# Eight tiles or six transposed on TensorE: tiles 6 and 7 moved to DMA transposes, with a new written order

## The chip, the cores and the metric

The kernel runs on one core of one Trainium2 chip. The metric is the device time of one execution in microseconds, the median of three runs.

## What is computed

Attention with four batches, eight heads, 768 positions and a head width of 64, in which each position sees the first 8 positions and the last 96 up to itself, followed by a two-layer network with a squared ReLU:

```python
scores = scale * np.matmul(q, k.transpose(0, 1, 3, 2))
keep = is_global | is_local          # pos < 8, or 0 <= rel < 96
bias = -slopes[:, None, None] * dist[None, :, :]
a = softmax(np.where(keep, scores + bias, -1e9))
attn = np.matmul(a, v)               # (4, 8, 768, 64)
x = attn.transpose(0, 2, 1, 3).reshape(3072, 512)
h = x @ w_in                         # (3072, 2048)
g = np.maximum(h, 0.0) ** 2
out = g @ w_out                      # (3072, 512)
```

## The kernel before

The 3072 rows are cut into 24 tiles of 128 (`j`, six for each batch) and 12 blocks of two tiles (`blk`). Because a position sees at most 96 back, a tile's scores need only its own keys and those of the tile before it; the first 8 keys and values of a batch are copied into each later tile (`gk`, `gv`, or a copy `kl`).

The program first builds a list of operations (`Plan.op`), each with the engines that may do it, and then emits them one after the other in the sequence that the string `ORDER` gives (`Plan.run`). A word of `ORDER` is the name of an operation; `:` is followed by the PSUM banks that it takes, `@A`, `@V` or `@P` picks ACT, DVE or POOL, `#2` the second operation of that name. Each engine works through its own operations strictly in this sequence, so `ORDER` is the order of PE, ACT, DVE, and of the two lines of transfers, POOL's and SP's. Nothing else sets it: the planner's keys and costs in the code are not used for the order. Numbers such as `LEADS` and `key=` only describe.

The operations, in the course of a tile:

- `ld.q.j`, `ld.k.j`, `ld.v.j`, `ld.win.s.c`, `ld.wout.s` (line 307) and `load.j` (line 310: v, q and k of tile j, from tile 6 on) are loads issued by POOL, with the cast to bf16. q and k of tile 0 come from SP as float32 (`plain`, line 319). The weights are loaded in eight steps `s` of 256 columns or rows; steps 0 and 2 of w_in in two halves.
- `tr.0.j` and `tr.1.j` (line 506) transpose q and k of tile j on PE, four 128x128 transposes each, and `T.0.j`, `T.1.j` (lines 429 to 433) copy them from a bank to `qkT`. This holds for `j < JQK`. For later tiles `T.j` (line 537) is one DMA transpose of q and k together, issued by SP.
- `bias.j` (line 579, first three tiles) and `sc.j` (line 599) fill the banks with scores, `exp.j` (line 665, ACT) and `mul.j` (line 690, DVE) make the weights, `pv.j` (line 748) multiplies with v, `norm.j` (lines 778 and 779, DVE) divides.
- `trx.j` (line 816) and `xT.j` (lines 429 to 433) transpose the result x on PE for `j < JX`; for later tiles `xT.j` (line 840) is a DMA transpose issued by SP.
- `s1` and `relu`, `sq` (lines 1061, 865, 1098) are the first layer for blocks 0 and 1. From block 2 on it is done by seven products of half size in place of eight: `isum` and `xs` (lines 888 and 922) are sums of weights and inputs, `h` (line 950) the products, `u`, `c` and `q` what ACT and DVE make of them.
- `s2.0` (line 1339) is the second layer for block 0, with `w_out` step by step; from block 1 on it is seven products too: `wsum` and `sum` (lines 1132 and 1167) are sums of w_out and hidden values, `s2.blk.p1` to `p7` (line 1212) the products, `part` and `o` (lines 429 and 1287) what collects them, `st` (lines 1309 and 1381) the stores, issued by SP.
- `warm` (line 532) is eight matmuls of zeros. The same eight run once at the very start (line 372).

The waits that matter around the change: `s2.0.s.sub` waits for `ld.wout.s`, `wsum.i.g` for four steps of w_out, `isum.i.g` for the transposes `tr` of all tiles of the first loads and for four steps of w_in, `T.j` for the landing of `load.j`, and `load.j` for the transposes that free its place in the ring of three q and k buffers.

Of the kernel before, what the change touches and what calls it, by code (L numbers as in the profile page):

```python
# [77 lines left out]
isum.1.0 T.8 s2.0.6.1 u.2.1.2@A s2.0.6.0 isum.3.0 pv.6.1:0 h.2.0.p6 wsum.2.1 wsum.0.1 s2.1.p1.1 s2.0.7.1 c.2.1.c11
norm.6.0 gate.13 o.0.1@V st.0.1 s2.0.7.0 h.2.1.p7 part.1.p1@A s2.1.p6.0 u.2.0.2@A o.0.0@A u.2.1.3@A h.2.0.p7 h.2.1.p4
T.9 norm.6.1 wsum.3.0 u.2.0.3@A sc.7.0:1762 c.2.1.c21@A wsum.1.1 h.2.1.p5:0 c.2.1.c22 q.2.1.c11@A s2.1.p2.0:4  # L80
exp.7.1.0 exp.7.0.0 isum.2.1 load.10 h.2.0.p4 exp.7.0.1 mul.7.0 exp.7.1.1 s2.1.p2.1 isum.2.0 s2.2.p1.0:7 q.2.1.c21@A
mul.7.1 h.2.0.p5:1 s2.1.p6.1 part.1.p6@A trx.6:6 gate.12 c.2.0.c21@A load.12 pv.7.0:2 xT.6@A c.2.0.c22 q.2.1.c22@A
q.2.0.c22@A s2.2.p1.1 h.2.1.p3 s2.1.p7.0 wsum.3.1 o.1.p2 norm.7.0 h.2.0.p3 pv.7.1:5 s2.1.p7.1 q.2.0.c21@A st.0.0
c.2.1.c12 s2.1.p5.0 s2.1.p5.1 part.1.p7@A q.2.1.c12@A s2.1.p4.0 T.10 s2.1.p4.1 c.2.0.c12 gk.7@V q.2.0.c12@A o.1.p5
o.1.p4@A sc.8.0:6201 st.1.1 part.2.p1@A s2.1.p3.0 norm.7.1 sum.2.0 sum.2.1 s2.1.p3.1 trx.7:5 xT.7@V o.1.p3 h.3.0.p1:3
exp.8.1.0 gk.8@V h.3.1.p1:2 exp.8.0.0 exp.8.1.1 exp.8.0.1 h.3.0.p2:6 xs.3.0 u.3.1.1@A sc.9.0:1540 s2.2.p6.0 mul.8.0
xs.3.1 mul.8.1 u.3.0.1@A h.3.0.p6 exp.9.0.1 exp.9.1.1 gv.7@V h.3.1.p2:4 c.3.0.c11 h.3.1.p6 c.3.1.c11 exp.9.0.0
pv.8.0:0 s2.2.p6.1 pv.8.1:6 load.11 norm.8.0 u.3.1.2@A s2.2.p2.0:1 sum.2.2 gv.8@P q.3.1.c11@A norm.8.1 xT.8 h.3.1.p7
h.3.0.p5:4 u.3.0.2@A h.3.0.p7 s2.2.p2.1 exp.9.1.0 st.1.0 part.2.p6@A xs.3.2 u.3.1.3@A q.3.0.c11@A h.3.1.p5:0 s2.2.p7.0
u.3.0.3@A mul.9.1 mul.9.0 s2.2.p7.1 c.3.1.c22 T.12 c.3.0.c22 pv.9.0:6 h.3.1.p3 o.2.p2 h.3.0.p4 c.3.1.c12 load.15  # L90
norm.9.0 q.3.1.c22@A h.3.0.p3 s2.3.p1.0:5 s2.3.p1.1 c.3.0.c12 q.3.0.c22@A pv.9.1:0 c.3.0.c21@A part.2.p7@A norm.9.1
q.3.1.c12@A h.3.1.p4 q.3.0.c12@A h.4.0.p1:3 c.3.1.c21@A s2.2.p5.0 part.3.p1@A gk.9@V sc.10.0:6402 s2.2.p5.1
q.3.0.c21@A sum.3.0 sum.3.1 s2.2.p4.0 s2.2.p4.1 exp.10.1.0 sum.2.3 exp.10.0.0 exp.10.0.1 h.4.0.p2:4 T.11 u.4.0.1@A
exp.10.1.1 gk.10@V gv.9@A s2.3.p6.0 o.2.p5 mul.10.0 c.4.0.c11 xT.9 h.4.1.p1:6 o.2.p4@A mul.10.1 s2.2.p3.0 s2.2.p3.1
q.3.1.c21@A s2.3.p2.0:0 sum.3.2 u.4.1.1@A pv.10.0:2 pv.10.1:4 s2.3.p6.1 xs.4.0 gate.17 o.2.p3 part.3.p6@A xs.4.1
s2.3.p2.1 norm.10.0 h.4.0.p6 h.4.1.p6 q.4.0.c11@A gv.10@A norm.10.1 u.4.0.2@A load.13 s2.3.p7.0 sc.11.0:7124 u.4.1.2@A
sum.3.3 h.4.0.p7 h.4.1.p7 xs.4.2 exp.11.1.0 o.3.p2 exp.11.0.0 u.4.0.3@V s2.3.p7.1 sc.12.0:17 exp.11.1.1 exp.11.0.1
gate.16 xT.10 h.4.0.p4 c.4.0.c21@A mul.11.0 st.2.0 mul.11.1 h.4.1.p2:4 c.4.1.c11 exp.12.1.0 s2.3.p5.0 pv.11.0:2
pv.11.1:3 s2.3.p5.1 norm.11.0 part.3.p7@A h.4.0.p5:7 q.4.1.c11@A u.4.1.3@A norm.11.1 h.4.1.p5:4 q.4.0.c21@A gate.20
s2.3.p4.0 c.4.0.c22 load.14 s2.3.p4.1 h.4.0.p3 T.13 gate.18 load.16 c.4.1.c22 exp.12.0.0 h.4.1.p4 q.4.1.c22@A h.4.1.p3  # L100
xT.11 s2.4.p2.0:2 h.5.0.p1:3 q.4.0.c22@A o.3.p5 mul.12.0 c.4.0.c12 o.3.p4@A c.4.1.c21@A u.5.0.1@A c.4.1.c12 T.15
s2.3.p3.0 q.4.0.c12@A s2.3.p3.1 q.4.1.c12@V q.4.1.c21@A h.5.0.p2:1 o.3.p3 sc.13.0:5764 st.3.1 st.2.1 h.5.1.p1:0
exp.13.0.0 T.14 s2.4.p2.1 c.5.0.c11 exp.13.1.0 pv.12.1:1 q.5.0.c11@A s2.4.p1.0:5 xs.5.0 sum.4.0 pv.12.0:7 xs.5.1
s2.4.p1.1 mul.13.0 h.5.0.p6 gk.13@V u.5.1.1@A exp.13.0.1 h.5.1.p6 exp.13.1.1 h.5.0.p5:6 sum.4.1 norm.12.0 norm.12.1
h.5.1.p2:4 xs.5.2 mul.13.1 c.5.1.c11 h.5.1.p5:7 u.5.1.2@A sum.4.2 gate.19 part.4.p1@A h.5.1.p7 u.5.0.2@A h.5.0.p7
o.4.p2 u.5.0.3@A c.5.0.c22 pv.13.0:1 u.5.1.3@A norm.13.0 s2.4.p6.0 s2.4.p6.1 xT.12 st.3.0 q.5.1.c11@A T.16 part.4.p6@A
h.5.0.p4 pv.13.1:4 s2.4.p5.0 sum.4.3 c.5.0.c21@A h.5.0.p3 h.5.1.p4 q.5.0.c22@A s2.4.p7.0 norm.13.1 s2.4.p7.1 s2.4.p5.1
c.5.0.c12 q.5.0.c21@A kl.15@V part.4.p7@A c.5.1.c22 q.5.0.c12@A sc.14.0:1346 o.4.p5 s2.4.p4.0 xT.13 exp.14.0.1 kl.14@V
h.5.1.p3 gv.13@P q.5.1.c22@V c.5.1.c12 c.5.1.c21@A s2.4.p4.1 load.17 h.6.0.p1:4 s2.4.p3.0 s2.4.p3.1 exp.14.1.1
exp.14.1.0 exp.14.0.0 sc.15.0:0673 mul.14.1 mul.14.0 xs.6.0 o.4.p4@A xs.6.1 h.6.0.p2:1 o.4.p3 q.5.1.c12@A s2.5.p1.0:5  # L110
u.6.0.1@A c.6.0.c11 exp.15.0.0 exp.15.1.0 exp.15.1.1 sum.5.0 s2.5.p1.1 h.6.0.p6 u.6.0.2@A exp.15.0.1 sum.5.1 load.18
h.6.0.p5:2 part.5.p1@A pv.14.0:0 norm.14.0 pv.14.1:6 h.6.1.p1:1 u.6.1.1@A h.6.0.p7 gv.14@P st.4.0 s2.5.p6.0 u.6.0.3@A
# [1319 lines left out]
```

## Time and profile before

| what | value |
|---|---|
| three runs | 199.76, 199.83 and 200.56 us |
| median | 199.83 us |
| span of the profiled execution | 197.6 us |
| instructions of PE, ACT, DVE, POOL in it | 2776, 335, 423, 101 |
| busy time of PE, DVE, ACT, POOL | 191.9, 173.2, 163.0, 80.4 us |
| loads by POOL (q0) | 13.37 MB in 80256 packets |
| stores and transposes by SP (q1) | 13.11 MB in 31570 packets |

The span runs from the first to the last instruction of one profiled execution; the page gives no other time for that execution, and the median of the runs is 2.2 us above the span. A matmul's shown time runs on into the next one's, so the step from one start to the next tells what a matmul costs, and the chain of waits gives these steps added up. In a timeline the columns are start, duration, engine, line and operation, what is written and read with its shape, the count of merged instructions, and in brackets the idle time before and what ended it. An issue of a transfer is shown on POOL or SP; its landing is told by the DMA view, as a median time from issue.

### The profile page before, as it was taken

The page shows a single profiled execution, that of the slowest core. Times are in us where ns is not written, and L with a number is a line of the kernel's source. Part 1 is how long each engine was busy: PE and PEld are TensorE (multiplying, and loading weights), DVE is VectorE, ACT ScalarE, POOL GpSimd, SP SyncE. Part 2 cuts the span into 40 slices and gives each one's busy share as a digit, 9 for nine tenths or more (in the row PEclk, how much of TensorE's full clock was granted, in tenths as well). Part 3 has the DMA queues.
Part 4 walks back from the last instruction along what each step waited for, and adds up shares of the span by engine and source line. Part 5 has one row for each costly group of instructions (what it writes and reads, how often), then busy time and mean ns, then how long its engine had stood idle before and what let it go on. Part 6 is the DMA issues. An engine that isn't in the chain of part 4 may idle for free.

```text
span 197.6 us, 6777 instructions
## 1 busy us (share of the span) xinstructions
PE 191.9 (97%) x2776; PEld 169.6 (86%) x2776; DVE 173.2 (88%) x423; ACT 163.0 (82%) x335; POOL 80.4 (41%) x101
## 2 busy tenths in 40 slices
PE   7989999999999999999999999999999999999993
...
DMA  6999999999999999999999999999695711114023
GB/s 127 153 158 171 181 181 185 182 202 159 139 209 191 75 200 88 145 174 210 151 129 203 114 124 194 160 121 92 136 81 116 154 55 56 27 30 163 0 106 106
DMA packets 111857, 26.91 MB, mean 136 GB/s; under 512 B 103379, under 2 KB 109011, under 8 KB 111827
## 3 DMA queue, kind: packets, MB, share of 16 engines
q0 software_dynamic: 80256, 13.37, 91.8%
q1 hardware_dynamic: 31570, 13.11, 32.5%
q8 instruction: 21, 0.34, 0.6%
q14 instruction: 10, 0.07, 0.1%
...
## 4 chain that ended last, share of the span: by engine, by line
PE 95%; DVE 2%; issue 1%; ACT 0%; DVEq 0%
PE bank L1212 35%; PE bank L950 32%; PE bank L1061 7%; PE bank L599 6%; PE bank L748 5%; PE bank L1339 4%; PE bank L372 2%; PE bank L506 2%; PE bank L532 1%; DVE qkT L433 1%; PE bank L816 1%; PE bank L579 0%; ACT qkT L429 0%; DVE o L1287 0%; DVE v L433 0%
## 5 line engine op out<-in xcount | busy, mean ns | idle before, releaser
L1015 ACT ACTIVATE hs<-hr 128x512 bf16<-128x512 f32 x72 | 44.8, 641 | 5.1 <-DVE hr L995 4.7
L665 ACT ACTIVATE esc<-bank 128x512 bf16<-128x512 f32 x78 | 42.9, 614 | 1.3 <-PE bank L599 1.0
L1212 PE MATMUL bank<-wsum,hsum 128*128 128x256 bf16 x264 | 36.2, 273 | 0.0
L1212 PEld LDWEIGHTS <-hsum 128*128 128x128 bf16 x360 | 32.1, 98 | 4.1 <-issue 0.5
L995 DVE CUSTOM_DVE_ANT_0 hr<-bank,early 128x512 f32<-128x512 f32 x45 | 30.4, 685 | 2.5 <-PE bank L950 1.5
L950 PEld LDWEIGHTS <-win 128*128 128x128 bf16 x480 | 29.7, 98 | 1.0
L950 PEld LDWEIGHTS <-qk_first 128*128 128x128 bf16 x480 | 29.7, 98 | 1.0
L429 ACT COPY early<-bank 128x512 f32<-128x512 f32 x42 | 24.5, 591 | 3.6 <-PE bank L950 3.3
L690 DVE TENSOR_TENSOR at<-esc,E 128x1024 bf16<-128x1024 bf16 x39 | 26.7, 696 | 0.1
L1212 PEld LDWEIGHTS <-hs 128*128 128x128 bf16 x264 | 24.0, 98 | 2.6
L310 POOL DMA_DIRECT2D qk<-in_q_dram x18 | 16.0, 890 | 21.9 <-DMA qkT<-qk 20.6
L1212 PE MATMUL bank<-wout,hs 128*128 128x256 bf16 x176 | 24.9, 273 | 0.0
L310 POOL DMA_DIRECT2D v<-in_v_dram x18 | 16.0, 888 | 18.3 <-DVE v L480 14.9
L950 PE MATMUL bank<-xT,win 128*128 128x128 bf16 x320 | 23.4, 219 | 0.0
L431 POOL COPY v<-v 8x520 bf16<-8x520 bf16 x8 | 5.7, 718 | 43.3 <-PE bank L748 43.3
L950 PE MATMUL bank<-xs,qk_first 128*128 128x128 bf16 x320 | 22.8, 219 | 0.0
L779 DVE TENSOR_TENSOR x<-bank,rs 128x256 bf16<-128x256 f32 x48 | 20.4, 425 | 1.7
L865 ACT ACTIVATE hr<-bank 128x512 f32<-128x512 f32 x33 | 19.4, 598 | 1.3 <-PE bank L950 0.4
L748 PE MATMUL bank<-v,at 128*128 128x65 bf16 x352 | 17.8, 193 | 0.0
L1287 DVE TENSOR_TENSOR o<-bank,part 128x256 f32<-128x256 f32 (+2 forms) x34 | 13.8, 410 | 3.3 <-PE bank L1212 3.2
L429 ACT COPY part<-bank 128x256 f32<-128x256 f32 x29 | 10.9, 375 | 7.1 <-PE bank L1212 6.9
L310 POOL DMA_DIRECT2D qk<-in_k_dram x18 | 16.1, 897 | 0.9 <-DMA win<-in_moe_w_in_dram 0.5
...
## 6 DMA issues: line engine op xcount, KB each, us to landing
out_dram<-o SPq DMA_DIRECT2D x22, 256.0 KB, 2.5
v<-in_v_dram POOLq DMA_DIRECT2D x24, 128.0 KB, 5.6
qk<-in_q_dram POOLq DMA_DIRECT2D x18, 128.0 KB, 5.0
qk<-in_k_dram POOLq DMA_DIRECT2D x18, 128.0 KB, 5.8
wout<-in_moe_w_out_dram POOLq DMA_DIRECT2D x8, 256.0 KB, 8.5
win<-in_moe_w_in_dram POOLq DMA_DIRECT2D x6, 256.0 KB, 6.9
qk_first<-in_k_dram POOLq DMA_DIRECT2D x5, 128.0 KB, 5.6
qk_first<-in_q_dram POOLq DMA_DIRECT2D x5, 128.0 KB, 5.7
```

What stands on the lines that cost most here:

```text
L310: nc.gpsimd.dma_start(out=dst, in_=src)
L429: nc.scalar.copy(dst, src)
L665: nc.scalar.activation(out=tiles[tag, j, g][:, odd], in_=tiles.pop(("sc", j, odd, g)).rearrange("p a c -> p (a c)"), func=Act.Exp, scale=s ...
L690: nc.vector.tensor_mul(at, tiles.pop(("esc", j, g)), bias)
L748: nc.tensor.matmul(out=po[:, hi, :], lhsT=tiles["at", j, g][:, odd, at * P : (at + 1) * P], rhs=v_sb[kj][:, h, :], start=(i == 0), stop=(i ...
L779: nc.vector.tensor_tensor(out=x[:, 4 * hf : 4 * hf + 4, :], in0=po[:, :, :D], in1=rs.to_broadcast([P, 4, D]), op=Alu.mult,)
L865: nc.scalar.activation(dst, src, Act.Relu)
L950: nc.tensor.matmul(out=tiles["h", blk, g, bank][:, n], lhsT=left_[:, s, k], rhs=right_[:, k], start=opens and n == 0 and k == 0, stop=k == ...
L995: nc.vector._custom_dve(TENSOR_ADD_SAT, out=hr, in0=src, in1=tiles.pop(("u", blk, g, i)), s0=float("inf"), s1=0.0,)
L1015: nc.scalar.activation(hs, hr, Act.Square)
L1061: nc.tensor.matmul(out=hT[:, c, cols], lhsT=w_in_sb[s][:, kt, c * P : (c + 1) * P], rhs=tiles["xT", blk][:, kt, cols], start=(kt == 0), st ...
L1212: nc.tensor.matmul(out=tiles["acc", blk, bank][:, cols], lhsT=left_[:, s], rhs=right_[:, cols], start=first and s == 0, stop=s == NSTEP - ...
```

## The change

Two constants say up to which tile transposes run on PE. They go from 8 to 6, so that tiles 6 and 7 take the path of the later tiles: `T.6` and `T.7` in place of four `tr` and four copies, and `xT.6`, `xT.7` as DMA transposes in place of two `trx` and two copies. All else that is computed stays as it is. `ORDER` is written anew from its first word to its last: the same operations (but for those of tiles 6 and 7) in another sequence, with other banks, and with some fifty copies and small operations given to another of the engines that may do them. Of the old and of the new order, the part up to the first product with w_out and the last lines:

```diff
--- before.py
+++ after.py
 ORDER = """
-tr.0.0:0 warm:7 tr.1.0:1 T.1.0@V bias.0.0:23 T.0.0@A sc.0.0 ld.win.3.0 exp.0.0.0 ld.k.1 tr.1.1:4 bias.1.0:5670 T.1.1@V ld.q.1
-tr.0.1:1 ld.v.0 exp.0.1.0 T.0.1@V sc.1.0 exp.1.0.1 pv.0.0:2 ld.q.2 tr.0.2:3 norm.0.0 ld.k.2 T.0.2@V ld.k.3 exp.1.1.1
-pv.0.1:4 tr.1.2:1 bias.2.0:7203 ld.v.1 norm.0.1 exp.1.1.0 ld.q.3 tr.1.3:6 gk.1@A T.1.2@A sc.2.0 exp.1.0.0 T.1.3@V
-ld.k.4 pv.1.0:4 ld.v.2 gk.2@V exp.2.1.0 exp.2.1.1 norm.1.0 trx.0:1 xT.0@A ones.6 pv.1.1:5 tr.0.3:6 T.0.3@V exp.2.0.0
-tr.1.4:2 ld.win.6.0 sc.3.0:4361 ld.q.4 norm.1.1 ld.v.3 trx.1:7 gv.1@V exp.2.0.1 exp.3.0.0 pv.2.0:5 exp.3.1.0 exp.3.0.1
-T.1.4@V xT.1@V pv.2.1:0 ld.k.5 ld.win.2.0 exp.3.1.1 gk.3@A ld.win.2.1 norm.2.0 s1.0.3:2 mul.3.0 s1.0.6:4 ld.win.4.0
-tr.0.4:7 ld.q.5 ld.v.4 norm.2.1 mul.3.1 relu.0.6@A s1.0.3#2 gv.2@P pv.3.0:3 norm.3.0 trx.2:5 T.0.4@A pv.3.1:6
-ld.win.1.0 norm.3.1 ld.win.0.1 xT.2@A sc.4.0:1047 exp.4.1.1 exp.4.1.0 tr.1.5:3 T.1.5@A s1.0.2:5 trx.3:6 xT.3@V
-ld.win.0.0 ld.win.5.0 s1.0.2#2 s1.0.2#3 s1.0.2#4 relu.0.3@V exp.4.0.1 ld.v.5 gv.3@P exp.4.0.0 gk.4@V sq.0.6@V
-relu.0.2@A s1.1.3:7 ld.win.7.0 relu.1.3@A load.6 s1.1.6:0 mul.4.1 tr.0.5:6 mul.4.0 sq.0.3@V s1.1.2:3 T.0.5@A ld.wout.3
-pv.4.0:2 ld.wout.1 sq.0.2@V sc.5.0:4157 ld.wout.0 s1.0.4:6 relu.1.2@A exp.5.1.1 s1.0.1:3 sq.1.3@A exp.5.0.0 relu.0.4@V
-s1.1.4:7 ld.wout.2 norm.4.0 pv.4.1:4 gv.4@P norm.4.1 sq.0.4@A load.7 exp.5.1.0 sq.1.2@A relu.1.4@A s1.0.0:6 gate.9
-ld.wout.4 mul.5.0 s1.0.0#2 sq.1.4@A s1.0.0#3 s1.1.5:2 trx.4:1 exp.5.0.1 relu.1.6@V s1.1.1:4 ld.wout.5 s1.0.1#2
-relu.1.1@A E0.1 mul.5.1 relu.1.5@A pv.5.0:7 s1.1.7:0 s1.1.0:5 sq.1.1@V norm.5.0 ld.wout.6 E0.0 sq.1.5@V tr.1.6:4
-sq.1.6@A pv.5.1:2 relu.1.7@A tr.0.6:7 s1.0.0#4 norm.5.1 xT.4@A sq.1.7@A h.2.0.p2:0 ld.wout.7 T.1.6@V h.2.1.p2:1
-trx.5:2 xT.5@V relu.1.0@A sq.1.0@A gate.14 h.2.0.p1:5 xs.2.0 s1.0.5:4 sum.1.2 s1.0.7:2 relu.0.1@A xs.2.1 gate.10
-sum.1.0 sum.1.1 relu.0.0@A T.0.6@A sc.6.0:36 wsum.0.0 sum.1.3 sq.0.0@A sq.0.1@A s2.0.0.0:7 relu.0.7@A s2.0.1.0 load.9
...
-part.11.p6@A s2.11.p2.0:6 st.10.1 s2.11.p2.1 sum.11.2#2 o.11.p2 s2.11.p7.0 s2.11.p7.1 part.11.p7@A sum.11.3 s2.11.p5.0
-s2.11.p5.1 o.11.p5 st.11.1 st.11.0 sum.11.3#2 s2.11.p4.0 s2.11.p4.1 o.11.p4@A st.11.1#2 s2.11.p3.0 s2.11.p3.1
-s2.11.p3.0#2 o.11.p3 s2.11.p3.1#2 st.11.0#2 o.11.p3#2 st.11.0#3
+ld.q.1 ld.win.7.0 ld.win.2.0 ld.k.1 ld.q.2 ld.k.3 tr.0.0:4 tr.1.1:7 tr.0.1:5 warm:1 ones.6 T.0.0@A tr.1.0:0 T.0.1@A
+T.1.1@A T.1.0@A ld.q.3 ld.k.2 ld.v.0 ld.v.1 ld.q.4 ld.win.3.0 ld.win.6.0 ld.win.1.0 ld.win.0.0 ld.v.2 ld.k.4 ld.win.2.1
+ld.q.5 ld.v.3 ld.win.4.0 ld.win.0.1 ld.k.5 load.6 ld.wout.3 ld.win.5.0 ld.v.4 ld.wout.5 ld.wout.6 load.7 ld.wout.7
+ld.v.5 ld.wout.2 ld.wout.1 ld.wout.0 ld.wout.4 tr.1.3:6 tr.0.2:3 tr.1.2:4 bias.0.0:52 sc.0.0 exp.0.1.0 T.1.2@A exp.0.0.0
+T.0.2@V T.1.3@V bias.1.0:3610 sc.1.0 tr.0.3:2 exp.1.1.1 exp.1.1.0 exp.1.0.0 exp.1.0.1 pv.0.0:4 T.0.3@V bias.2.0:7205
+pv.0.1:3 norm.0.0 gk.1@V norm.0.1 sc.2.0 pv.1.0:4 exp.2.0.0 exp.2.0.1 exp.2.1.1 exp.2.1.0 trx.0:1 pv.1.1:3 gk.2@V
+norm.1.0 norm.1.1 gv.1@V xT.0@V gate.9 sc.3.0:7406 tr.0.4:5 tr.1.4:3 exp.3.0.0 trx.1:2 pv.2.0:1 pv.2.1:7 T.1.4@V
+exp.3.1.0 xT.1@V gk.3@A exp.3.1.1 exp.3.0.1 T.0.4@A gv.2@A s1.0.3:3 mul.3.0 norm.2.0 mul.3.1 norm.2.1 s1.0.6:4 s1.0.2:2
+s1.0.2#2 s1.0.2#3 s1.0.2#4 pv.3.0:0 pv.3.1:6 trx.2:7 tr.0.5:5 s1.0.3#2 norm.3.0 norm.3.1 relu.0.6@A relu.0.2@A
+sc.4.0:1402 xT.2@A T.0.5@A tr.1.5:6 trx.3:5 s1.0.4:7 sq.0.6@A exp.4.0.0 exp.4.1.0 exp.4.1.1 relu.0.4@A exp.4.0.1
+sq.0.2@A gate.12 gv.3@V xT.3@V gk.4@V relu.0.3@V T.1.5@V s1.1.6:5 T.6 load.8 sc.5.0:3642 s1.0.1:1 s1.0.1#2 s1.1.2:7
+mul.4.0 sq.0.4@V mul.4.1 isum.0.1 E0.1 exp.5.0.0 exp.5.1.0 pv.4.0:6 relu.1.6@A sq.0.3@A relu.1.2@A exp.5.0.1 relu.0.1@A
+s1.1.1:3 s1.0.0:5 pv.4.1:0 s1.1.7:7 s1.0.0#2 s1.0.0#3 s1.0.0#4 s1.1.3:4 sq.1.2@A isum.0.0 gate.11 E0.0 mul.5.0 sq.1.6@V
+norm.4.0 relu.0.0@V sq.0.1@A gv.4@A relu.1.7@A exp.5.1.1 sq.1.7@V norm.4.1 isum.3.1 relu.1.3@V sq.0.0@A s1.0.7:1
+relu.0.7@A relu.1.1@A s1.1.4:2 trx.4:0 s1.1.5:6 sq.0.7@A xT.4@A sq.1.3@A relu.1.4@A mul.5.1 pv.5.0:7 isum.1.0 sq.1.1@V
+s1.1.0:4 s1.0.5:1 pv.5.1:5 relu.1.5@A sq.1.4@A relu.1.0@A wsum.0.0 norm.5.0 gate.10 isum.1.1 isum.2.1 norm.5.1
+s2.0.0.0:2 h.2.0.p1:6 sc.6.0:47 u.2.0.1@A exp.6.0.0 wsum.1.0 s2.0.0.1:3 s2.0.1.1 h.2.1.p2:0 trx.5:4 exp.6.1.0 sq.1.0@A
...
+sum.11.2#2 o.10.p5 s2.10.p3.0 s2.10.p3.1 part.11.p6@V o.10.p3 sum.11.3#2 sum.11.3 s2.11.p5.0 s2.11.p7.0 s2.11.p7.1
+s2.10.p4.1 s2.11.p5.1 st.10.0 o.10.p4@V st.11.0 st.10.1 part.11.p7@A s2.11.p4.0 s2.11.p4.1 o.11.p4@A o.11.p5 s2.11.p3.0
+s2.11.p3.1 o.11.p3 s2.11.p3.0#2 s2.11.p3.1#2 o.11.p3#2 st.11.1 st.11.1#2 st.11.0#2 st.11.0#3
 """
...
     NSPLIT = 4
     NBIAS = 3
-    JQK, JX = 8, 8
+    JQK, JX = 6, 6
     JGATE = 9
```

In the new order POOL's line begins with q1, w_in 7, the first half of w_in 2, k1, q2, k3, q3, k2, v0, v1, q4, and has all of its first 40 loads without a copy between them, ending with w_out 7, v5, and w_out 2, 1, 0 and 4. PE begins with the transposes of q of tile 0, k and q of tile 1, then `warm`, then k of tile 0. SP's line begins with `T.6 T.7 T.8 st.0.1 xT.6 T.9 st.0.0 xT.7`. The copies gv.2, gv.4, gv.8 and gv.16 go from POOL to ACT, gv.3 from POOL to DVE.

176 lines of the change are left out of this document (86 added, 90 removed).

## The prediction

> **What bounds the kernel now.** I read the page first: the busy shares, the slices, the queues and the chain.
>
> ```profile
> span 197.6 us, 6777 instructions
> ...
> PE 191.9 (97%) x2776; PEld 169.6 (86%) x2776; DVE 173.2 (88%) x423; ACT 163.0 (82%) x335; POOL 80.4 (41%) x101
> ...
> PE   7989999999999999999999999999999999999993
> ...
> DMA  6999999999999999999999999999695711114023
> ...
> q0 software_dynamic: 80256, 13.37, 91.8%
> ...
> PE 95%; DVE 2%; issue 1%; ACT 0%; DVEq 0%
> ```
>
> TensorE is the bound: 97% busy, 95% of the chain that ended last, and it is busy 90% or more in every slice from the third to the last but one. So PE work removed comes off the end, and a wait of PE goes onto it. The second thing to see is the DMA row: full from slice 2 on, nearly all of it q0, the queue into which POOL puts its loads. Does PE run ahead of its loads or close behind them? For that I took PE's timeline:
>
> ```profile
> 1.19 3.60 PE L372 MATMUL bank<-early 128*128 128x512 bf16 x8 [1.19 <-DVE early L361]
> 4.58 1.06 PE L506 MATMUL bank<-ident,plain 128*128 128x128 f32 x4
> 5.43 2.62 PE L532 MATMUL bank<-early 128*128 128x512 bf16 x8
> ...
> 9.28 0.40 PE L599 MATMUL bank<-qkT 64*128 64x128 bf16 x8 [0.34 <-DVE qkT L433]
> ...
> 38.59 0.40 PE L599 MATMUL bank<-qkT 64*128 64x128 bf16 x8
> 38.92 3.63 PE L1339 MATMUL bank<-wout,hs 128*128 128x512 bf16 x16
> ```
>
> The first scores (sc.0.0) start at 9.28 and the first product with w_out (s2.0.0.0, L1339) at 38.92. Then POOL's timeline, which holds the issues of the loads:
>
> ```profile
> 1.34 0.89 POOL L307 DMA_DIRECT2D win<-in_moe_w_in_dram  x1 [0.17 <-issue]
> 2.22 0.90 POOL L307 DMA_DIRECT2D qk_first<-in_k_dram  x1
> 3.10 0.90 POOL L307 DMA_DIRECT2D qk_first<-in_q_dram  x1
> ...
> 10.88 0.86 POOL L307 DMA_DIRECT2D win<-in_moe_w_in_dram  x1
> 11.63 1.00 POOL L307 DMA_DIRECT2D qk_first<-in_q_dram  x1
> ...
> 29.04 1.55 POOL L307 DMA_DIRECT2D wout<-in_moe_w_out_dram  x2 [0.45 <-DMA win<-in_moe_w_in_dram]
> ...
> 36.33 0.70 POOL L307 DMA_DIRECT2D wout<-in_moe_w_out_dram  x1 [0.56 <-DMA wout<-in_moe_w_out_dram]
> 37.61 0.71 POOL L307 DMA_DIRECT2D wout<-in_moe_w_out_dram  x1 [0.58 <-DMA wout<-in_moe_w_out_dram]
> ```
>
> and the DMA view of four narrow windows, whose last column is the time from issue to landing: the load of k1 (issued 2.22), of wout.0 (29.04), of wout.6 (36.33) and of wout.7 (37.61), in this order:
>
> ```profile
> qk_first<-in_k_dram POOLq DMA_DIRECT2D x1, 128.0 KB, 5.7
> ```
> ```profile
> wout<-in_moe_w_out_dram POOLq DMA_DIRECT2D x1, 256.0 KB, 8.3
> ```
> ```profile
> wout<-in_moe_w_out_dram POOLq DMA_DIRECT2D x1, 256.0 KB, 8.7
> ```
> ```profile
> wout<-in_moe_w_out_dram POOLq DMA_DIRECT2D x1, 256.0 KB, 8.7
> ```
>
> A load takes 5.7 us at the start and 8.7 at the end, and POOL itself waits half a microsecond per issue for an earlier load to land. So q0 is a backlogged line: a load lands when all the bytes ahead of it have passed. Landing times are 7.9 (k1), 37.3 (wout.0), 45.0 (wout.6) and 46.3 (wout.7). PE took up wout.0 only 1.6 us after it landed. **Before, PE already runs just behind its loads.** What counts in the new order is therefore each load's place in that line.
>
> **The change part by part.**
>
> *The transposes.* Gone from PE are four groups tr.0.6, tr.1.6, tr.0.7, tr.1.7 and trx.6, trx.7, four 128x128 transposes each. The chain in order of time has them as
>
> ```profile
> 42.55 0.45 PE bank L506 x8
> ...
> 49.79 0.90 PE bank L950 x16
> 50.69 0.55 PE bank L599 x16
> ...
> 54.44 0.22 PE bank L816 x4
> ```
>
> 0.45 for two groups and 0.22 for one: six times 0.22 is **1.3 us off the path**. Six copies out of the banks go too (four on ACT, two on DVE); neither engine is on the path, so I count them at nothing. Added are two DMA transposes of q and k, T.6 and T.7, first in SP's line, and two of x, xT.6 and xT.7, behind T.8 and T.9. SP is free for them; its first work behind the opening loads was
>
> ```profile
> 51.49 1.34 SPq L537 DMA_TRANSPOSE qkT<-qk  x1
> ```
>
> xT.6 and xT.7 are hidden by some 5 us of PE work that stands between the norms of a tile and the first difference xs of block 3. T.6 and T.7 run on the DMA engines in the very stretch in which q0 is backlogged. Their own size, and how the line bears them:
>
> ```profile
> qkT<-qk SPq DMA_TRANSPOSE x16, 3.8
> xT<-x SPq DMA_TRANSPOSE x16, 3.2
> ...
> GB/s 175 177 198 179 164 156 138 110 109 105 175 163 154 161 155 157 150 137 147 158 211 250 274 298 314 312 288 328 325 234 233 188 184 205 220 248 266 282 218 197
> ```
>
> The last row is 82 to 86 us in 0.1 us steps, with one T and one xT beside loads. A T moves 256 KB; at about 215 GB/s (an estimate from the middle of this row) it is 1.2 us of all engines, two are 2.4 us. Sums of 300 show that some of it fits beside the loads. Ends: 0 and 2.4 us later for every load behind them; I take the middle, 1.2.
>
> The Trainium skill, "DMA: Bandwidth & Descriptors", section "Queues, rings and completion order", says that each DMA engine goes round between the queue rows that have work, a packet at a time. By that rule a T is not put behind the backlog, it cuts in at once, and q0 pays: the sum would take the end of 2.4. The row agrees that it cuts in, and shows rates above those of q0 alone.
>
> *The start.* The new order puts k1's transpose second on PE, ahead of the eight warm matmuls and of k0, and k1 itself behind q1, win.7.0 and win.2.0. By POOL's rows (0.88 from one issue to the next, 0.75 behind a later win) k1 is issued at 3.7 and lands at 9.4 or later, where PE stood ready at 5.6. Then tr.0.1, warm (2.4, from the end of the row ahead of L532's to that of L532's own), tr.1.0 (0.45), the three transposes of k3, q2, k2 and the bias (0.45): sc.0.0 at about 13.9, 4.6 later than 9.28, with 2.4 us less PE work behind it (five groups done early, six gone). That alone is **+2.2 us**.
>
> *The loads.* POOL's first 40 loads are the same in both orders (22 of q, k and v, ten of w_in, eight of w_out), and load.8 or load.9 follows. In the old order wout.3, 1, 0, 2 come 30th to 33rd of the 40, ahead of load.7; in the new one wout.2, 1, 0, 4 are the last four, with load.7 and v5 ahead of them. The line's length doesn't change with its order, so the last load lands at 46.3 as before and wout.0, one before it, at 45.0 (1.3 is the step between the last two rows above). With T.6 and T.7 it is 46.2, between 45.0 and 47.4. The copies gv.2 to gv.4 that leave POOL save issue time, not line.
>
> PE issues in order, and s2.0.0.0 needs wout.0. Could PE come there later than 46 anyway? The loads it needs on the way are late too; the last of them, v5 (36th), lands near 41 to 42 (three steps of 1.3 ahead of wout.0, with or without a transpose's toll), with 2.3 us of PE work from pv.5.0 to s2.0.0.0, so PE is there at 43 to 44.5 and **waits 1.5 to 3 us**. The start's 4.6 us lie inside this.
>
> *What stands behind the wait.* On PE everything. On DVE wsum.0.0 waits for the same load, and norm.5.0, two isums and norm.5.1 queue behind it:
>
> ```profile
> 39.52 0.68 DVE L1132 TENSOR_TENSOR wsum<-wout 128x1024 bf16<-128x1024 bf16 x1
> ```
> ```profile
> 35.40 0.16 DVE L778 RECIPROCAL rs<-bank 128x4 f32<-128x4 f32 x1
> 35.60 0.42 DVE L779 TENSOR_TENSOR x<-bank,rs 128x256 bf16<-128x256 f32 x1
> ```
>
> Five steps of about 0.6 are 3.1 us until trx.5 may start; PE has 2.5 us to do until then: two h of 0.45 (half of L950's 0.90 above), sc.6.0 with half of L599's 0.55, three s2 of 0.43 or 0.44 (an eighth of L1339's 3.63, less its tail). **+0.7 us**; if DVE has nothing left in front, 0.
>
> *Sum at s2.0.0.0.* Start moves from 38.92 to 46.2: +7.3. Behind it in the new order lie h.2.0.p1, h.2.0.p2, h.2.1.p2, sc.6.0 and trx.5, which were ahead of it (1.8 us), and four of the removed groups no longer do (0.9): +0.9. With trx.5's wait: 7.3 + 0.9 + 0.7 = **+8.9 us**. The rest of PE's line, and its end, I take as packed as before. The last rows of it were
>
> ```profile
> 194.57 0.28 PE L1212 MATMUL bank<-wout,hsum 128*128 128x64 bf16 x4 [0.45 <-DVE o L1287]
> ```
>
> and the new end has the same wait for the copy, with two matmul groups behind it in place of one and one fewer ahead. The stores of block 10 move some 2.6 us nearer to the end: 0 to 0.5, taken as 0. The span goes to 206.5. The median is 2.2 above the profiled span, and I carry that: **208.7 us**.
>
> The Trainium skill, "TensorE: Matmul & The Clock Gate", Part 1, says that PE falls to half its clock after an idle window of some 3.4 us. PE would idle 3.8 us or more for k1, and the eight warm matmuls come right behind. By that rule warm takes 3.6, as the first eight did (0.45 each), and sc.0.0 starts 1.2 later, inside the wait for wout.0; an idle of over 3.4 us there would add up to 1.7. The rows of before agree only on the cold start; their granted clock reads 1.00 there all the same.
>
> **The rivals.**
>
> *Start only.* Loads land 5.7 us after issue whatever stands ahead. By issue times wout.0 then lands at 32.2 + 5.7 = 37.9, and only the late sc.0.0 counts: 202.0. For it: 5.7 holds through the first 10 us. Against: 8.3 and 8.7 later, and POOL's waits. Chance 0.08.
>
> *Faster.* The same unloaded line, and PE makes good the late start on its way to w_out. Place: s2.0.0.0; it decides from 38.0 (38.92 less the 0.9 of work moved behind): if PE starts it earlier, the kernel is faster, and with the whole 1.3 us of transposes gone it takes 198.5. For it: PE is the bound and has less to do. Against: wout.0 would have to land 7 us ahead of the line. Chance 0.07.
>
> *Line without toll.* T.6 and T.7 fit wholly beside the loads, and some of PE's small waits vanish because DVE and ACT have caught up: its stretch from 38.92 to its end is 155.9 us, its matmuls in that stretch, at the steps of the chain, add up to 153.2, and I give back 1.5 of the difference: 8.9 - 1.2 - 1.5 = 6.2, 206.0. Chance 0.25.
>
> *Full toll.* The transposes cost the line 2.4 us and PE resumes at half clock: 8.9 + 1.2 + 1.7, 211.6. Chance 0.08.
>
> **How the numbers follow.** The forecast of 208.7 has 0.50; within 0.5% of no change (about what a measurement of this kernel can tell) I put 0.02. The range takes in the forecast with both ends of the toll, the line without toll less another 2.4 us for a line that moves faster than I read it, 203.6, and full toll at the upper end: 203.6 to 211.8. Left out are start only, faster and same, 0.17 in all, and little more. Faster 0.07, same 0.02, slower 0.91.
>
> **What would show it.** L1339's first matmul at 45 to 47 us, with idle time of PE before it put down to w_out's load; tr.1.1 at 9.4 or later; wout.0 landing over 8 us after issue; sc.0.0 near 14; trx.5 with a short wait for DVE; beyond 50 us PE full as before. Wrong would be the forecast if w_out's last loads land before 40, or if PE's remaining stretch, from s2.0.0.0 to its end, is shorter than the old 155.9 us.

## The result, and the profile after

The changed kernel takes 223.38 us, the median of four runs (222.33 to 224.27). The kernel before, on the same chip, takes 199.95 (199.76 to 200.56). The ratio is 1.1173, with a 95% interval of 1.1124 to 1.1223: slower, by 23.4 us. The forecast was 208.7, with 211.8 as its upper end. Some runs of a kernel lie in a slower state, over 1.5% above its fastest run: they enter the medians and ranges here and below, but not the ratios, so that the two can differ.

The page of the profiled execution of the changed kernel, with the same rows as before:

```profile
span 222.5 us, 6731 instructions
...
PE 198.9 (89%) x2752; PEld 172.1 (77%) x2752; DVE 175.0 (79%) x430; ACT 160.5 (72%) x324; POOL 78.7 (35%) x99
...
PE   7396989699999699993999899799999999998993
...
PEclk9799999889999999998599999999999999999999
DMA  8999999999179979999999499999996330130213
...
PE 34%; DMA 32%; DVE 18%; POOL 10%; issue 5%; SPq 0%; DVEq 0%; POOLq 0%
```

PE had 95% of the chain before and has 34% now; DMA has 32%. TensorE no longer sets the time alone. PE's row has several slices below 9, the deepest of them, besides those of the start and the end, about halfway, and right behind it the granted clock falls to 5 tenths. PE's timeline shows what it waited for (the rows with the longest idle times, and the first scores):

```profile
9.38 1.03 PE L504 MATMUL bank<-ident,qk_first 128*128 128x128 bf16 x8 [3.87 <-DMA qk_first<-in_k_dram]
...
14.51 0.40 PE L597 MATMUL bank<-qkT 64*128 64x128 bf16 x8
...
42.95 0.60 PE L746 MATMUL bank<-v,at 128*128 128x65 bf16 x8 [2.17 <-DMA v<-in_v_dram]
47.12 0.60 PE L1337 MATMUL bank<-wout,hs 128*128 128x512 bf16 x2 [0.23 <-DMA wout<-in_moe_w_out_dram]
...
75.80 0.60 PE L1210 MATMUL bank<-wsum,hsum 128*128 128x256 bf16 x4 [1.80 <-DVE part L431]
...
105.31 0.29 PE L597 MATMUL bank<-qkT 64*128 64x128 bf16 x2 [3.43 <-DMA qkT<-qk]
...
201.54 1.05 PE L948 MATMUL bank<-xs,qk_first 128*128 128x128 bf16 x16 [0.97 <-DVE xs L920]
```

Up to 47.12 this is close to the forecast: k1's transpose at 9.38 (9.4 or later), sc.0.0 at 14.51 (near 14), the first product with w_out at 47.12 (46.2). Beyond it come waits that the forecast didn't have: at 75.80 for a copy on DVE, at 105.31 for the DMA transpose of tile 13, and several of about 1 us, the last at 201.54. (Lines are two lower than before: 597 are the scores, 1210 the second layer, 948 the first.)

To see where the time goes, I take the start of each tile's scores and add all PE work still to come, at the durations of the prediction (0.45 for a product of either layer, 0.55 for a tile's scores and so on). The sum is the time at which PE would be done if it never waited again. Where it grows, time is lost.

| scores of tile | before | after | lost so far |
|---|---|---|---|
| 0 | 189.5 | 192.3 | 2.8 |
| 6 | 192.0 | 201.4 | 9.4 |
| 12 | 192.8 | 204.5 | 11.7 |
| 14 | 193.0 | 211.0 | 18.0 |
| 23 | 194.1 | 216.7 | 22.6 |
| span | 197.6 | 222.5 | 24.9 |

The profiled execution was the slowest of the four, so its 24.9 stand for the 23.4 of the medians. The loss at tile 6, 9.4, is what was forecast for all of the kernel (8.9). Another 13.2 come between tile 6 and tile 23, of which 6.3 lie between tiles 12 and 14, and 2.3 come at the end. For those around tile 13, the windows of the changed kernel on PE (busy time, granted clock, share and rate of DMA):

```profile
102.00:104.00 2.00, 0.00 (x0) 1.00 3.09 135
104.00:106.00 2.00, 0.69 (x14) 0.56 1.30 204
106.00:108.00 2.00, 2.00 (x21) 0.50 0.74 212
108.00:110.00 2.00, 2.00 (x21) 0.50 1.79 114
110.00:112.00 2.00, 2.00 (x23) 0.74 2.22 148
```

PE idles 3.43 us, and then works at half its clock until 111: of the 6.3 us, 3.43 are the wait and the other 2.9 the half clock: what PE does in the 5.7 us at 0.50 would take half as long at 1.00. The clock also fell behind the wait for v5, in front of the first product with w_out:

```profile
43.00:46.00 3.00, 3.00 (x21) 0.50 1.24 203
```

The DMA view in two narrow windows tells how long T.6 (issued at 30.30) and T.13 (98.31) took to land:

```profile
qkT<-qk SPq DMA_TRANSPOSE x1, 8.4
...
qkT<-qk SPq DMA_TRANSPOSE x1, 7.0
```

Before, the median was 3.8. The waits (total, times, longest), of the kernel before in the first row and of the changed kernel in the others, show the other end of this:

```profile
POOL qk L310 <- DMA qkT<-qk: 20.6, 4, 7.0
...
POOL qk L308 <- DMA qkT<-qk: 59.6, 6, 17.4
DVE xs L920 <- DMA xT<-x: 7.8, 6, 3.4
```

POOL stands 59.6 us, 20.6 before, in front of loads whose place in the ring of three a transpose still has to free, one of these waits 17.4 us long. Towards the end the chain has two stores whose buffer DVE's next copy waits for:

```profile
196.68 4.07 DMA out_dram<-o
...
215.07 2.02 DMA out_dram<-o
```

These are times to landing, not idle times. PE lost 0.97 us behind the first, in the row of 201.54 above, as DVE came to that xs late. Behind the second PE's rows show no idle time, and DVE itself was idle for only 0.43 us in front of its copy.

### The profile page after: what moved, and what is told of

It reads as the page before. It is cut to its first block, busy times and chain, and to the rows that moved or that the text cites. A ratio compares the mean times of both kernels' runs of the same rounds, so it can differ in the third digit from the quotient of the medians.

```text
span 222.5 us, 6731 instructions
## 1 busy us (share of the span) xinstructions
PE 198.9 (89%) x2752; PEld 172.1 (77%) x2752; DVE 175.0 (79%) x430; ACT 160.5 (72%) x324; POOL 78.7 (35%) x99
## 4 chain that ended last, share of the span: by engine, by line
PE 34%; DMA 32%; DVE 18%; POOL 10%; issue 5%; SPq 0%; DVEq 0%; POOLq 0%
PE bank L948 17%; PE bank L1210 14%; DMA wout<-in_moe_w_out_dram 8%; DMA xT<-x 8%; DMA out_dram<-o 5%; DMA qkT<-qk 5%; DMA v<-in_v_dram 4%; POOL qk_first L305 3%; DVE hr L993 3%; POOL win L305 2%; DVE wsum L1130 2%; DVE x L777 2%; DVE hsum L1165 2%; DMA qk<-in_k_dram 2%; PE bank L746 2%
## 5 line engine op out<-in xcount | busy, mean ns | idle before, releaser
L1013 ACT ACTIVATE hs<-hr 128x512 bf16<-128x512 f32 x69 | 42.0, 638 | 4.9 <-DVE hr L993 4.6
L1210 PEld LDWEIGHTS <-hsum 128*128 128x128 bf16 x360 | 32.9, 98 | 8.6 <-issue 4.6
L308 POOL DMA_DIRECT2D qk<-in_q_dram x18 | 16.0, 887 | 60.5 <-DMA qkT<-qk 59.6
L1210 PE MATMUL bank<-wsum,hsum 128*128 128x256 bf16 x264 | 35.2, 273 | 2.1 <-DVE part L431 1.8
L427 ACT COPY early<-bank 128x512 f32<-128x512 f32 x42 | 24.6, 591 | 15.1 <-PE bank L948 14.1
L948 PEld LDWEIGHTS <-win 128*128 128x128 bf16 x480 | 31.0, 100 | 1.9 <-issue 0.2
L948 PE MATMUL bank<-xs,qk_first 128*128 128x128 bf16 x320 | 24.1, 222 | 2.1 <-DVE xs L920 1.8
L948 PE MATMUL bank<-xT,win 128*128 128x128 bf16 x320 | 24.2, 226 | 0.0
L746 PEld LDWEIGHTS <-at 128*128 128x128 bf16 x352 | 15.5, 98 | 4.8 <-issue 3.9
L597 PE MATMUL bank<-qkT 64*128 64x128 bf16 x192 | 14.0, 222 | 3.7 <-DMA qkT<-qk 3.4
L1059 PE MATMUL bank<-xT,win 128*128 128x256 bf16 (+1 forms) x160 | 16.8, 263 | 0.0
```

What stands on the lines that cost most here:

```text
L308: nc.gpsimd.dma_start(out=dst, in_=src)
L427: nc.scalar.copy(dst, src)
L746: nc.tensor.matmul(out=po[:, hi, :], lhsT=tiles["at", j, g][:, odd, at * P : (at + 1) * P], rhs=v_sb[kj][:, h, :], start=(i == 0), stop=(i ...
L948: nc.tensor.matmul(out=tiles["h", blk, g, bank][:, n], lhsT=left_[:, s, k], rhs=right_[:, k], start=opens and n == 0 and k == 0, stop=k == ...
L1013: nc.scalar.activation(hs, hr, Act.Square)
L1059: nc.tensor.matmul(out=hT[:, c, cols], lhsT=w_in_sb[s][:, kt, c * P : (c + 1) * P], rhs=tiles["xT", blk][:, kt, cols], start=(kt == 0), st ...
```

## The experiments

Times are medians with the range of the runs; three kernels have one run alone. "Old order" is that of the kernel before. Ratios are to the kernel before, on the same chip.

| kernel | what it is | us | ratio, 95% interval |
|---|---|---|---|
| a_loads | changed, first 40 loads in old sequence | 217.4 | one run |
| b_pool | changed, later loads in order of tiles | 229.8 | one run |
| b_sp | changed, T.9 to T.15 ahead of an xT | 228.5 | one run |
| d_alone | old order, constants 6 and 6 | 213.8 (213.3 to 214.0) | 1.0713 (1.0667 to 1.0759) |
| d_qk | old order, only T.6 and T.7 | 207.1 (204.8 to 209.1) | 1.0336 (1.0271 to 1.0402) |
| d_x | old order, only xT.6 and xT.7 | 208.3 (206.2 to 209.4) | 1.0398 (1.0336 to 1.0460) |
| d_hold | d_alone, six loads held back | 209.3 (207.6 to 210.4) | 1.0476 (1.0418 to 1.0533) |
| d_t7 | old order, only T.7 | 199.95 (198.8 to 200.8) | 1.0021 (0.9993 to 1.0048) |
| e_tensor | new order, tiles 6 and 7 on TensorE | 218.5 (216.3 to 219.0) | 1.0926 (1.0845 to 1.1007) |
| e_both | e_tensor, first 40 loads in old sequence | 216.0 (213.2 to 217.1) | 1.0737 (1.0630 to 1.0843) |
| f_13 | changed, load 13 ahead of load 14 | 220.8 (218.9 to 221.7) | 1.1052 (1.0996 to 1.1107) |
| g_fill | d_x, PE kept busy in the wait | 205.8 (205.1 to 206.6) | 1.0305 (1.0270 to 1.0340) |
| h_after | changed, warm inside the wait for k1 | 224.5 (218.6 to 225.7) | not told apart |
| h_warm | e_both, the same | 215.8 (214.6 to 216.9) | 1.0836 (1.0780 to 1.0891) |
| h_warm13 | h_warm, and load 13 ahead | 218.4 (213.2 to 220.0) | not told apart |

**The sequence of the first loads.** a_loads gives them the old one, at the head of the order:

```diff
-ld.q.1 ld.win.7.0 ld.win.2.0 ld.k.1 ld.q.2 ld.k.3
+ones.6 ld.win.3.0 ld.k.1 ld.q.1 ld.v.0 ld.q.2
...
-load.7 ld.wout.7 ld.v.5 ld.wout.2 ld.wout.1 ld.wout.0 ld.wout.4
+ld.wout.3 ld.wout.1 ld.wout.0 ld.wout.2 load.7 ld.wout.4 ld.wout.5 ld.wout.6 ld.wout.7
```

> The changed kernel (223.4 us) with POOL's first 40 loads in the old sequence, all else as changed. Theory Q, two losses that add: the place of w_out in the line of loads costs 7 to 8 us up to the first product with w_out, and the rest is lost later, on the lines of POOL and SP, whatever happened before. It expects that product to start at 39 to 41 us in place of 47.1, and about 216 us. Rival P, all that is late later follows from the first 47 us: 201 to 206 us. Rival D, the transposes of tiles 6 and 7 by DMA are the burden: within 2 us of 223.

217.4: by this one run, 6 us of the 23.4 are the sequence of loads, and over 17 are something else. The first product with w_out starts at 40.67 with no wait, but sc.6 now waits for its transpose, and the later waits are still there:

```profile
42.67 0.40 PE L597 MATMUL bank<-qkT 64*128 64x128 bf16 x8 [0.97 <-DMA qkT<-qk]
```

**Unblocking POOL or SP.** POOL waits 17.4 us for a place in the ring with load 12, ahead of loads 10 and 11 whose places are free; SP holds T.9 behind xT.6. b_pool and b_sp put these in order of the tiles:

```diff
-load.9 T.9 load.12 st.0.0 ... load.10 ... T.10 load.11 ... load.14 load.13
+load.9 T.9 load.10 load.11 load.12 st.0.0 ... T.10 ... load.13 load.14
```
```diff
-sc.5.0:3642 ... st.0.1 xT.6 ... load.9 T.9 load.12 st.0.0 xT.7 ... load.10 ... T.10 ... xT.8 st.1.1 T.11
+sc.5.0:3642 load.9 ... st.0.1 T.9 xT.6 ... load.12 load.10 st.0.0 xT.7 ... T.10 ... T.11 xT.8 st.1.1
```

> The changed kernel with the loads of tiles 8 to 23 in the order of the tiles (before: 12 ahead of 10 and 11, 14 ahead of 13, 21 ahead of 20), all else as changed. Theory Q1, POOL is stopped by load.12, which waits for T.9, and takes loads 10 and 11 with it: they go out at about 49 us in place of 68, T.10 some 15 us earlier, and the kernel takes 215 to 219 us. Rival Q2, SP's line holds the transposes T back behind xT: POOL only waits one load later, 221 to 224 us.

> The changed kernel with T.9 to T.15 ahead of the xT (and the store) that stood in front of each in SP's line; POOL's line as changed. Theory Q2, T.9 behind xT.6 keeps a place in the ring of q and k, and POOL waits 17.5 us for it: the wait falls to 5 to 7 us, PE's idle of 3.4 us ahead of the scores of tile 13 goes, and the kernel takes 211 to 216 us. Rival Q1, the order of the loads decides: 220 us or more. Rival P: no change, 222 to 224 us.

Both theories fell: 229.8 and 228.5, slower than the changed kernel. Each is a single run. 228.5 lies in the open range of rival Q1, that the order of the loads decides, but b_pool speaks against it. In b_pool load 13 now waits 23.47 us, and the loads behind it go out in one burst at 95 to 103. POOL's row names PE, but what came just before it is the gate, a small write on DVE at 94.02. In b_sp the transposes that were moved ahead hold SP for their loads, and the xT behind them are late (POOL's, DVE's and then PE's timeline):

```profile
94.62 0.88 POOL L308 DMA_DIRECT2D v<-in_v_dram  x1 [23.47 <-PE bank L948]
```
```profile
94.02 0.06 DVE L478 MEMSET v<- 128x1 bf16 x1
```
```profile
109.37 0.95 PE L948 MATMUL bank<-xT,win 128*128 128x128 bf16 x8 [4.91 <-DMA xT<-x]
```

POOL's waits for the ring did get shorter, 37.8 us in b_pool and 43.3 in b_sp in place of 59.6, and the kernel is slower all the same: their sum isn't what sets the time.

**The transposes alone, in the old order.** d_alone changes the two constants and only the words of tiles 6 and 7:

```diff
-    JQK, JX = 8, 8
+    JQK, JX = 6, 6
...
-tr.1.6:4 ... tr.0.6:7 ... T.1.6@V ... T.0.6@A ... trx.6:6 ... xT.6@A
+T.6 ... xT.6
```

> The old order with only tiles 6 and 7 moved: T.6, T.7, xT.6 and xT.7 in place of their transposes on TensorE, at the places of those, the constants at 6. Theory Q, the transposes are no burden by themselves: PE loses 1.3 us of work, 198.0 to 200.0 us. Rival D, transposes among the opening loads delay w_out, and xT.6 and xT.7 come late for block 3: 201 to 206 us.

213.8, above both theories. Most of the loss is in two waits and in half clock behind the second, in PE's timeline and, for the second, in the chain:

```profile
41.87 0.40 PE L597 MATMUL bank<-qkT 64*128 64x128 bf16 x8 [2.96 <-DMA qkT<-qk]
...
73.63 1.04 PE L948 MATMUL bank<-xs,qk_first 128*128 128x128 bf16 x8 [7.62 <-DVE xs L920]
```
```profile
63.68 8.56 DMA xT<-x
```

A transpose of x that took 3.2 us in the middle before takes 8.56 here. Its issue lies among loads 12 and 11, which POOL issues at 58 to 66. That gave theory L: a transpose issued while loads are under way lands late. Four kernels take it apart: d_qk and d_x have one kind each, d_t7 has T.7 alone, and d_hold holds the loads back behind the operation that needs xT.7:

```diff
-gate.11 ... gate.12 load.12 ... xT.7 ... h.3.0.p2:6 xs.3.0
+xT.7 ... h.3.0.p2:6 xs.3.0 gate.12 load.12 gate.11
```

> Old order, x of tiles 6 and 7 back on TensorE, only q and k of the two tiles by DMA transpose. Theory L (a transpose lands with the loads that are under way when it is issued, and PE waits for it): only the wait of sc.6 for T.6 is left, about 3 us as before, less 0.9 us of removed PE work: 201.5 to 203.5. Theory P (all four DMA transposes cost alike, through the room that they take): half of the loss, 206 to 207.

> Old order, q and k of tiles 6 and 7 back on TensorE, only x of the two by DMA transpose. Theory L: the wait of block 3's first product for xs and so for xT.7 stays, 6 to 8 us, with some 2.5 us at half clock behind it, less 0.4 us: 207 to 210.5. Theory P: half of the loss, 206 to 207.

> Old order, all four transposes by DMA, but the gates of loads 11 and 12 and load 12 stand behind xs.3.0, so that these six loads can't be under way beside xT.7. Theory L: xT.7 lands 3 to 5 us after issue in place of 8.6, PE waits 2 to 4 us in place of 7.6 and doesn't fall to half clock: 204.5 to 208.5. Theory P: the transposes cost what they cost, and loads 11 and 12 come later besides: 213 to 216.

> Old order, only q and k of tile 7 by DMA transpose. Theory L: T.7 has over 10 us until sc.7 needs it, so its late landing costs nothing, and 0.45 us of PE work is gone: 199.2 to 200. Theory P: a quarter of the loss, 202.5 to 203.5.

d_x came out as L has it: xT.7 takes 9.72 us (chain), and PE waits 8.07 (timeline).

```profile
59.82 9.72 DMA xT<-x
```
```profile
70.85 1.03 PE L948 MATMUL bank<-xs,qk_first 128*128 128x128 bf16 x8 [8.07 <-DVE xs L920]
```

d_qk misses L's range and lies 0.1 above P's, but not for P's reason: most of its loss is one wait, 5.97 us long and so twice that of d_alone, because T.6 took 10.36 us (timeline, then chain).

```profile
44.51 0.61 PE L597 MATMUL bank<-qkT 64*128 64x128 bf16 x8 [5.97 <-DMA qkT<-qk]
```
```profile
34.10 10.36 DMA qkT<-qk
```

In d_hold xT.7 lands in 4.3 us (DMA view), and PE waits 2.55 for it in place of 7.62:

```profile
xT<-x SPq DMA_TRANSPOSE x1, 4.3
```
```profile
69.74 1.03 PE L948 MATMUL bank<-xs,qk_first 128*128 128x128 bf16 x8 [2.55 <-DVE xs L920]
```

The time is 0.8 above L's range and 4.5 below d_alone. Half clock still follows this wait, and the wait for T.6, which nothing was done about, came out longer than the 2.96 of d_alone:

```profile
41.70 0.40 PE L597 MATMUL bank<-qkT 64*128 64x128 bf16 x8 [4.01 <-DMA qkT<-qk]
```

So the loads under way are what makes xT.7 late; for T.6 this wasn't tried. By their times alone, d_qk and d_x, each about half of the loss of d_alone, would fit P as well; d_hold and d_t7 speak against it. d_t7 says where a DMA transpose is harmless: T.7 is issued at 41.27 and takes 7.7 us, its scores come at 50.32 with no wait, and the time doesn't move by what can be measured. It is not a gain either, though 0.45 us of PE work is gone; none of the versions beats the kernel before.

**The clock behind a wait.** g_fill puts 30 matmuls, whose result nobody reads, into the wait of d_x:

```diff
-sc.9.0:1540 s2.2.p6.0
+fill:4 sc.9.0:1540 s2.2.p6.0
```

> As the kernel with x of tiles 6 and 7 alone by DMA (old order), with 30 matmuls of nothing in a free bank ahead of sc.9, some 6.5 us of PE work that ends before xT.7 lands. Theory C (the wait of 8.1 us has an echo, PE at a granted clock of 0.50 until 3.5 us after it): the clock stays at 1.00 from 62 to 76 us and the kernel takes 206 to 207.2. Rival (what is lost behind the wait comes from DVE and ACT): no change, 208 to 209.

Theory C held, at 0.2 below its range. The windows of d_x, then those of g_fill (busy, granted clock, DMA):

```profile
68.00:71.00 3.00, 0.15 (x2) 0.50 1.14 71
71.00:74.00 3.00, 3.00 (x33) 0.50 0.00 0
```
```profile
68.00:71.00 3.00, 1.90 (x35) 1.00 0.19 12
71.00:74.00 3.00, 3.00 (x57) 1.00 0.02 5
```

In the same 3 us PE gets through 57 matmuls in place of 33. Of d_x's loss about 2 us are the echo of the wait, not the wait: 2.4 by the medians (208.3 less 205.8), 1.9 by the ratios, whose intervals just overlap.

**The order alone.** e_tensor is the new order with tiles 6 and 7 back on TensorE; e_both has the old sequence of the first loads too. In both, isum and u no longer wait for the transposes of tiles 6 and 7, as these stand behind the first of them in this order.

```diff
-    JQK, JX = 6, 6
+    JQK, JX = 8, 8
...
-T.6 ... s2.0.0.0:2 ... T.7 ... xT.6 ... xT.7
+tr.0.6:0 T.0.6@A tr.1.6:3 T.1.6@A s2.0.0.0:2 ... tr.0.7:5 T.0.7@A ... tr.1.7:5 T.1.7@A ... trx.6:1 xT.6@A ... trx.7:6 xT.7@V
```

> The new order with q, k and x of tiles 6 and 7 transposed on TensorE again, put where PE passes anyway (tile 6 while it waits for w_out, the rest beside T.7, xT.6 and xT.7). Theory L (what is lost behind 50 us comes from late DMA transposes of tiles 6 and 7 and from those queued behind them): s2.0.0.0 stays at 46 to 47.5, the waits behind it shrink: 209 to 214. Rival O (the order itself lays its loads and transposes too close together, whichever tiles are on DMA): 218 to 223.

> As the kernel before it, with the first 40 loads in their old sequence besides: nothing is left of the change but the new order behind the loads. Theory L: 201 to 206. Rival O: 211 to 217.

Theory L fell here, and O held. With no transpose of tiles 6 and 7 on DMA the new order still loses 18.8 us (218.5 less 199.7). With the old loads in front it loses 16.3 by the median and 14.7 by the ratio (0.0737 of 199.7). What in the order does it, the sequence, the banks or the copies given to other engines, these two kernels don't tell apart.

Theory L missed one more thing: the first product with w_out came at 44.91, not at 46 to 47.5 (PE's timeline of e_tensor).

```profile
44.91 0.60 PE L1339 MATMUL bank<-wout,hs 128*128 128x512 bf16 x2 [1.00 <-DMA wout<-in_moe_w_out_dram]
```

The loads stand in the same sequence as in the changed kernel, where this load let PE go at 47.12. Without T.6 and T.7 it landed 2.2 us earlier.

T.13 is late in e_tensor just the same (PE's timeline):

```profile
104.98 0.23 PE L599 MATMUL bank<-qkT 64*128 64x128 bf16 x2 [3.17 <-DMA qkT<-qk]
```

In e_both, PE's losses by the same sums as above are 4.5 us at tile 0, 5.4 at tile 6, 10.1 at tile 12, 14.5 at tile 14 and 17.0 at tile 23. Some of them aren't DMA at all:

```profile
56.31 0.61 PE L950 MATMUL bank<-xs,win 128*128 128x128 bf16 x8 [1.16 <-ACT u L428]
...
71.30 0.61 PE L950 MATMUL bank<-xT,win 128*128 128x128 bf16 x8 [0.90 <-DVE o L432]
...
102.97 0.29 PE L599 MATMUL bank<-qkT 64*128 64x128 bf16 x2 [2.69 <-DMA qkT<-qk]
```

**Taking the order apart.** T.13 waits for load 13, which stands behind load 14 on POOL, and load 14 waits 14 us for its place in the ring. f_13 turns the two round in the changed kernel and moves the gate ahead:

```diff
-gate.14 ... gate.13 ... load.14 load.13
+gate.14 gate.13 ... load.13 load.14
```

> The changed kernel with one thing moved: load 13 stands ahead of load 14 on POOL, and its gate further ahead on DVE, so that it doesn't wait with POOL for T.11. Theory H (the 3.4 us wait of sc.13 for T.13, and the half clock behind it, come from load 13 standing behind load 14, which waits 14 us for its place in the ring): T.13 is issued some 5 us earlier, the wait of sc.13 is under 0.5 us and no half clock follows: 216.5 to 218.5. Rival Q (the loads that are let go earlier make the next transposes late, and the wait returns there): 221.5 to 224.5.

220.8, between the two: 2.6 us better by the medians, where wait and half clock were 6.3 in the changed kernel's profile. The wait of sc.13 is gone, but two others came, for an xT in front of it and for T.15 behind it (PE's timeline):

```profile
92.13 1.07 PE L948 MATMUL bank<-xs,qk_first 128*128 128x128 bf16 x16 [1.34 <-DVE xs L920]
...
117.64 0.23 PE L597 MATMUL bank<-qkT 64*128 64x128 bf16 x2 [1.72 <-DMA qkT<-qk]
```

h_after, h_warm and h_warm13 move the eight warm matmuls to the front, into the wait for k1; the last has f_13's edit too:

```diff
-tr.0.0:4 tr.1.1:7 tr.0.1:5 warm:1
+tr.0.0:4 warm:1 tr.1.1:7 tr.0.1:5
```

> The changed kernel with the eight warm matmuls moved from behind the wait for k1 into it. Theory of the prediction (the late start lies inside the wait for w_out): sc.0.0 starts 2 to 3 us earlier, s2.0.0.0 stays at 46.5 to 47.5 and the time at 222.5 to 224.5. Rival S (the start counts): 220 to 221.5.

> The new order with the old sequence of loads and tiles 6 and 7 on TensorE (216.0 us as measured), and the eight warm matmuls moved into the wait for k1. No wait for w_out is left there, so the start counts: 212.5 to 214. Rival (DVE and ACT set the pace behind it anyway): 215.3 to 216.5.

> As the kernel before it, with load 13 ahead of load 14 and its gate further ahead besides. Theory H (of the 16 us that the new order loses without any change to tiles 6 and 7 and to the first loads, 2.7 us are the wait for T.13 and 1.7 us the half clock behind it): 208 to 210.5. Rival Q (the wait returns at a later transpose): 211.5 to 214.

h_warm gained nothing that shows (215.8 beside 216.0; the intervals of the ratios overlap), and not for the rival's reason: PE comes to the next transposes earlier and waits there for k3 instead.

```profile
12.17 1.17 PE L505 MATMUL bank<-ident,qk_first 128*128 128x128 bf16 x12 [2.56 <-DMA qk_first<-in_k_dram]
```

In h_after sc.0.0 didn't come earlier either (14.6), so that it doesn't test whether a late start counts; its runs lie 7 us apart besides. In h_warm13 the wait for T.13 is gone, and xs waits 2.63 and 1.79 us in its place, for xT.9 and later ones:

```profile
90.18 1.89 PE L950 MATMUL bank<-xs,qk_first 128*128 128x128 bf16 x16 [2.63 <-DVE xs L922]
...
107.09 0.62 PE L950 MATMUL bank<-xs,qk_first 128*128 128x128 bf16 x8 [1.79 <-DVE xs L922]
```

The traces are as Q has it: in this order a wait that is taken away at one transpose comes back, in part or in full, at another. The time of h_warm13 tells nothing, as its runs lie 6.8 us apart.

## Why the prediction was wrong

**Right: the line of loads, and the first 50 us.** The start, the place of w_out in q0 and the wait in front of s2.0.0.0 came as worked out: 47.12 for 46.2, and 9.4 us lost at tile 6 for 8.9. Within it some details were off. Of the forecast wait of 1.5 to 3 us most was spent one step earlier, 2.17 for v5; PE then worked at half clock until about 46 and waited only 0.23 there. The toll of T.6 and T.7 on the loads was taken as 1.2, the middle of 0 and 2.4, and measured 2.2 (47.12 less 44.91, by e_tensor). a_loads bears out the cause, with 6.0 us in its one run.

**Wrong: "The rest of PE's line, and its end, I take as packed as before."** This is the step that failed. It put the whole new order behind s2.0.0.0 at nothing and gave no reason for it, and the run lost 13.2 us there and 2.3 at the end. e_both shows that the order itself does it: it has the old first loads and none of the moved transposes, and loses 14.7 to 16.3 us. Which of its parts does how much isn't shown. Read from its trace, but not tested apart, are the late start (4.5 by tile 0), T.13 with the half clock behind it (4.4 between tiles 12 and 14), and small waits for ACT's and DVE's copies. Where one was tested, by f_13, waits of 1.34 and 1.72 us came in place of the 3.43, and 2.6 us were gained. Which sequence of POOL, SP and DVE would free this order of its waits stays open.

**Wrong: "xT.6 and xT.7 are hidden by some 5 us of PE work", and T.6 and T.7 priced as a toll on the loads alone.** I had priced the transposes by what they do to the loads (0 to 2.4 us) and not by what the loads do to them. d_alone shows this error by itself: 14.1 us (213.8 less its 199.7), where PE has 1.3 us less to do. A cover of 5 us would have been enough for the 3.2 of the profile, and isn't for 8.56. That 3.2 and the 3.8 of T are medians. The view of 82 to 86 us, whose rates I read as "it cuts in", has this row as well, for the T issued in it, which nothing waited for:

```profile
qkT<-qk SPq DMA_TRANSPOSE x1, 6.5
```

The rule of the Trainium skill that I leaned on, "DMA: Bandwidth & Descriptors", section "Queues, rings and completion order", is that each engine goes round between the rows that have work; I read it as "it cuts in at once, and q0 pays". That q0 pays is what the runs show, with 2.2 us. That a transpose gets through at once they don't show: T.6 took 8.4 us. In the changed kernel itself this error is smaller. Tile 6's scores come after the wait for w_out, T.6 has landed by then, and putting tiles 6 and 7 back on TensorE (e_tensor) gains 4.9 us. Of the late xT.7 there is the 1.80 us in front of 75.80. The cover was 5.0 us as forecast (PE went idle at 74.00), but xT.7 took 5.46 (chain), and two xs and a copy on DVE come between it and PE:

```profile
68.98 5.46 DMA xT<-x
```

**The two errors don't add up.** 18.8 for the new order with its loads (e_tensor) and 14.1 for the transposes (d_alone) would be 32.9; the change costs 23.4. With the old first loads, the new order takes 213.2 to 217.1 without the transposes and 217.4, a single run, with them. I read this as a PE that is late for another reason and so gives the transposes their time; no run tests it.

**The end.** The stores of block 10 were seen to move nearer to the end, at "0 to 0.5, taken as 0". That came out within its bounds: PE's rows show no idle time for the store that lands at 217.09. Of the 2.3 us lost behind tile 23, 0.97 are the wait at 201.54, behind an earlier store of 4.07 us, which the prediction didn't have.

**The clock.** The prediction had half clock only at the start and in one rival. At the start it came, and the eight warm matmuls took 2.65 us (10.21 to 12.86), between its 2.4 and 3.6. Behind most of the waits of 2 us and more it came too, at about 2 us for one of 8.1 us (g_fill) and 2.9 for the one of 3.43, and so it belongs into the price of a wait.
